# Bias and mask of two more attention units added to the scores by TensorE, with the bias tile kept in unused k slots

## The chip, the cores and the metric

One core of one Trainium2 chip runs the kernel. The metric is device microseconds (us) of one execution. Five things matter on a core: TensorE (PE in the profile, its weight loads PEld), VectorE (DVE), ScalarE (ACT), GpSimd (POOL, which here only issues loads), SyncE (SP, which issues stores and transposing DMAs), and the 16 DMA engines behind the queues.

## What is computed

Sliding-window attention with a linear distance bias (ALiBi), then a SwiGLU feed-forward block on its output. Eight sequences of 576 positions, 8 heads of 64, a window of 128:

```python
scores = scale * np.matmul(q, k.transpose(0, 1, 3, 2))
bias = slopes[:, None, None] * (-np.abs(rel).astype(np.float32))[None, :, :]
mask = (rel >= 0) & (rel < window)
scores = np.where(mask, scores + bias[None], -1000000000.0)
attn = softmax(scores)              # with 1e-9 added to the sum
x = (attn @ v).reshape(4608, 512)
out = (silu(x @ w_gate) * (x @ w_val)) @ w_out
```

The inputs q, k, v, the three weights (512x1536, 512x1536, 1536x512) and the output are float32; the loads that GpSimd issues turn them into fp16.

## The kernel before

**Attention in units.** A unit is a tile of 128 keys with the 256 queries that can see it, for all 8 heads; 36 units in all, nine for each pair of sequences (the ninth holds the last 64 positions of both). A unit goes through these steps:

- `load_qk`, `load_v` (L182 to L196): loads of its tiles, each called by its *rank*, issued by GpSimd in an order written out by hand for ranks up to 10 (L876 to L908). Ranks 9 and 10 stand at the end of it, behind the weights.
- `transposed` (L198): four TensorE transposes into PSUM (`pt`) and one copy to the tile's home, by VectorE for q, by ScalarE for k from rank 4 on. Home of a k tile is slot `rank % 12` of `kT` (L113), a tile of 12 slots of 128x512 fp16. Ranks from 11 on are transposed by DMA. Slot 11 is read as zeros by idle matmuls at the start (L115).
- `scores` (L243): for a unit 256 queries wide, eight matmuls of 64x256 into four PSUM banks (`ps`), four exponentials on ScalarE (`act`, L282) into `ex`, and two multiplications on VectorE (`mul`, L286) of 128x1024 each by `reg`, a tile that holds exp(-slope x distance), with 0 outside the window. Units 3, 7 and 8 are narrower and go through `scores_128` (L295, `psc`, `exc`).
- `weighted` (L325): matmuls of the exponentials with v and a column of ones (`av`), a reciprocal and a multiplication on VectorE (`x`).
- `x_transposed` (L358): four TensorE transposes (`px`) and a ScalarE copy into `xT`, the feed-forward block's input.

**The first units.** For the units below `FIRST = 4` (L29), bias and mask are not multiplied in behind the exponential. `first_masks` (L98) writes -slope x distance / scale (with a distance of 16000 outside the window) into the tile `bias`, 128 x 8 x 256 fp16, and `products` (L267) begins each of the four PSUM banks with a matmul of the identity `idm` and 512 columns of `bias` (L273), onto which the products of k and q are added. `early_tile` (L263) chooses between the two ways: with it, four matmuls of 128x512 more and no `mul`.

**Space.** `bias` comes from the pool `hpool` with the tag `hT`, two buffers: `stage` (first inputs and distances) takes the first, `bias` the second, and the feed-forward block's `hT` tiles follow in turn.

**Feed-forward in blocks** of 512 tokens. Block 0 holds units 0 to 3, block 1 units 4 to 7. For each of 12 column groups m, `wide` (L389) does four matmuls for the gate (`pg`) and four for the value (`pv`) into a ring of three PSUM buffers with the tag `gv`; `gate` (L407) is a tanh on ScalarE (`tt`) and one VectorE operation (`uu`); `val` (L419) one more on VectorE, into `hT`. A PSUM buffer of the ring is free again when VectorE has read it. The output product is `project` (`po`, L446, 12 matmuls) for block 0, and `strassen` with fewer products for later ones.

**Order.** Up to step 8 of the feed-forward block the order on TensorE, VectorE and ScalarE is the program's (L940); from there to step 60 a scheduler places each engine's instructions by its own estimate of when they can start; from step 60 TensorE's order is the program's again (L952). GpSimd's order is by hand throughout. Each engine executes its list in order.

Of the kernel before, what the change touches and what calls it, by code (L numbers as in the profile page):

```python
# [11 lines left out]
FP16 = mybir.dt.float16  # L12
# [4 lines left out]
P = 128  # L17
# [9 lines left out]
IDLE = {("k", 0): 0, ("q", 0): 2}  # L27
REPEAT = {("q", 1): 4, ("k", 1): 2}
FIRST = 4  # L29
LEAD = 6  # L30
PRE = 0
SEVEN_FROM = 6
# [19 lines left out]
def kernel(  # L52
# [11 lines left out]
    B, H, S, D = q.shape  # L64
# [10 lines left out]
    hpool = ctx.enter_context(tc.tile_pool(name="hp", bufs=2))  # L75
# [16 lines left out]
    reg = consts.tile([P, H, 256], FP16, name="m_reg")  # L92


    bias = hpool.tile([P, H, 256], FP16, name="bias", tag="hT")
    by_slot = sorted(range(H), key=slot)

    def first_masks():  # L98
# [14 lines left out]
    kT = consts.tile([P, NK, 4, P], FP16, name="kT")  # L113
    qT = consts.tile([P, NQ, 4, P], FP16, name="qT")
    idle = kT[:, NK - 1].rearrange("p j t -> p (j t)")  # L115
    nc.vector.memset(idle, 0.0)


# [51 lines left out]
    def transposed_home(name, rank):  # L170
        return kT[:, rank % NK] if name == "k" else qT[:, rank % NQ]
# [26 lines left out]
    def transposed(name, rank):  # L198

        if rank < FIRST:  # L200
            pt = ps_f.tile([P, 4, P], FP32 if (name, rank) in hw else FP16, name="pt",
# [14 lines left out]
        for _ in range(REPEAT.get((name, rank), 1)):  # L216
            for j in range(4):
                nc.tensor.transpose(pt[:, j, :], t_[:, 2 * j:2 * j + 2, :],
                                    idm if rank < FIRST else idm2)
        if name == "k" and rank >= FIRST:  # L220
            nc.scalar.copy(transposed_home(name, rank), pt)
# [21 lines left out]
    def scores(i):  # L243

        s, p = units[i]
        def combined(n):
            return scores_128(s, (3, 7, 8)[n], 8, (s, "c", n), msk[n])

        def together(one, two):
            return [one[0] + two[0]] + one[1:] + two[1:]  # L250

        if p == 8:
            first = combined(0) if s == 0 else []
            return first + together(combined(1), combined(2))
        if p == 7 and s == 0:
            return scores_128(s, p, p, (s, p), reg[:, :, 0:P])
        if p == 7:
            return together(scores_128(s, p, p, (s, p), reg[:, :, 0:P]), combined(0))
        if p == 3:
            return scores_128(s, p, p, (s, p), reg[:, :, 0:P], i < FIRST)  # L260
        ks = (9 * s + p) % NK
        banks = []
        early_tile = i < FIRST  # L263
        e = epool.tile([P, H, 256], FP16, name="ex", tag="ex", bufs=4)
        ex[(s, p)] = e

        def products():  # L267
            for q4 in range(2):
                two = [ps_a.tile([P, 2, 256], FP32, name="ps", tag="a") for _ in range(2)]
                banks.append(two)  # L270
                for par in range(2 if early_tile else 0):
                    o = 4 * q4 + 2 * par
                    nc.tensor.matmul(two[par], idm, bias[:, o:o + 2, :], start=True, stop=False)  # L273
                for j in range(2):
                    pair = 2 * q4 + j
                    for par in range(2):
                        rows = slice(64 * par, 64 * par + 64)
                        nc.tensor.matmul(two[par][:, j, :], kT[rows, ks, pair, :],  # L278
                                         qT[rows, p:p + 2, pair, :], start=(j == 0 and not early_tile),
                                         stop=(j == 1))  # L280

        def act(q4, par):  # L282
            o = 4 * q4 + 2 * par
            nc.scalar.activation(e[:, o:o + 2, :], banks[q4][par], AF.Exp, scale=scale)  # L284

        def mul(q4):  # L286
            if early_tile:
                return
            o = slice(4 * q4, 4 * q4 + 4)
            nc.vector.tensor_mul(e[:, o, :], e[:, o, :], reg[:, o, :])  # L290

        return [[products], [lambda: act(0, 0)], [lambda: act(0, 1), lambda: mul(0)],
                [lambda: act(1, 0)], [lambda: act(1, 1), lambda: mul(1)]]

    def scores_128(s, kt, qt, key, m, early_tile=False):  # L295

        ks = (9 * s + kt) % NK
        banks = []
        e = epool.tile([P, H, P], FP16, name="exc", tag="exc", bufs=5)
        ex[key] = e  # L300

        er4 = e.rearrange("k (a par b) q -> k a par b q", a=2, par=2)

        def products():
            banks.extend(ps_a.tile([P, 4, P], FP32, name="psc", tag="a") for _ in range(2))
            for par in range(2 if early_tile else 0):
                nc.tensor.matmul(banks[par].rearrange("k (a b) q -> k a b q", a=2), idm,
                                 bias.rearrange("k (a par b) q -> k a par b q", a=2, par=2)
                                 [:, :, par, :, 0:P], start=True, stop=False)
            for j in range(4):  # L310
                for par in range(2):
                    rows = slice(64 * par, 64 * par + 64)
                    nc.tensor.matmul(banks[par][:, j, :], kT[rows, ks, j, :], qT[rows, qt, j, :],  # L313
                                     start=(j == 0 and not early_tile), stop=(j == 3))

        def act(par):
            nc.scalar.activation(er4[:, :, par], banks[par].rearrange("k (a b) q -> k a b q", a=2),  # L317
                                 AF.Exp, scale=scale)

        return [[products], [lambda: act(0)],  # L320
                [lambda: act(1), lambda: early_tile or nc.vector.tensor_mul(e, e, m)]]
# [3 lines left out]
    def weighted(i):  # L325
# [4 lines left out]
        for half in range(2):  # L330
            pool, tag = (ps_f, "gv") if i < FIRST else (ps_a, "a")
            av = pool.tile([P, 4, D + 1], FP32, name="av", tag=tag)
# [51 lines left out]
    hT = {}  # L384
# [424 lines left out]
    def first_tiles():  # L809

        first_masks()
        transposes_to(need[0] + 1)
        for n, _ in enumerate(run(scores(0))):
            if n == 0:
                transposes_to(need[1])
        for i in range(FIRST):
            if i + 1 < FIRST:
                for n, _ in enumerate(run(scores(i + 1))):
                    if n == 0 and i + 2 < FIRST:
                        transposes_to(need[i + 2])  # L820
            weighted(i)

            if i >= 2:
                begin(4, i - 1)
            if i > 0:
                x_transposed(i - 1)
        begin(6, 2)
        begin(4, 3)
        gate(0, 0, early[(0, 0, "g")][0], 0, 384)
        x_transposed(FIRST - 1)  # L830
        val(0, 0, early[(0, 0, "v")][0], 0, 384)
        later_masks(0, 2)
        gate(0, 1, early[(0, 1, "g")][0], 0, 384)
        val(0, 1, early[(0, 1, "v")][0], 0, 384)
        begin(6, 3)

    def attention():
# [3 lines left out]
        for _ in run(scores(FIRST)):  # L841
            yield FIRST
# [93 lines left out]
    def everything():  # L936
# [13 lines left out]
        for step in steps:  # L950
# [3 lines left out]
            if step == MASKS_AT:  # L954
# [3 lines left out]

            lead = LEAD if done < X_DMA_FROM - 2 else LEAD + 4
            blk = (0 if step + LEAD < b1 else 1 if step + LEAD < 60  # L960
                   else min(NBLK - 1, 2 + int((step + lead - 60) // 34.5)))
# [43 lines left out]
```

## Time and profile before

| | us |
|---|---|
| median of the 4 runs shown (344.7 to 345.17) | 344.94 |
| the profiled execution | 344.89 |
| its span, first to last instruction | 343.1 |

The profile is of one execution; its span leaves out 1.79 us ahead of the first instruction and behind the last. TensorE's granted clock was 1.000 throughout.

| engine | busy us | share of the span |
|---|---|---|
| PE | 329.5 | 96% |
| DVE | 277.7 | 81% |
| ACT | 207.7 | 61% |
| POOL | 109.8 | 32% |

How to read it: in a *timeline* each row is a run of like instructions of one engine, with its start, its length, and in square brackets how long the engine had been idle ahead of it and who ended that. Matmuls are pipelined: one of 128x512 is shown with 0.38 us, and the next starts 0.216 us later, so gaps are found by counting from start to start. A row's `out<-in` gives the tiles by the program's names, and L with a number is the line of the kernel.

### The profile page before, as it was taken

What the parts mean: (1) busy time and instruction counts of PE and PEld (TensorE: products, weight loads), DVE (VectorE), ACT (ScalarE), POOL (GpSimd) and SP (SyncE); (2) the same over time, 40 slices, a digit from 0 to 9 for tenths busy, and PEclk for the clock granted to TensorE, in tenths of its full rate; (3) what the DMA queues carried; (4) which work ended last, traced back from release to release, by engine and by line L of the source; (5) the groups of instructions that cost most, each with busy time, mean ns of one, the idle gap of its engine ahead of it and who ended that gap; (6) DMA issues with size and microseconds to landing.
All of it is one profiled execution on the core that took longest, in us unless ns stands there. A gap on an engine that the chain in (4) does not pass through costs nothing.

```text
span 343.1 us, 7778 instructions
## 1 busy us (share of the span) xinstructions
PE 329.5 (96%) x2983; PEld 218.7 (64%) x2983; DVE 277.7 (81%) x652; ACT 207.7 (61%) x412; POOL 109.8 (32%) x136
## 2 busy tenths in 40 slices
PE   7999989999999999999999999999999999999995
PEld 4484455444456566556565655565788878888884
DVE  6578886999798679988899999999855875775683
ACT  3758676465666765756556547563467666776640
POOL 8968672648765176743017000000000000000000
PEclk9999999999999999999999999999999999999999
DMA  9999999999999999999949914021101101011014
GB/s 153 169 180 176 162 171 148 85 129 167 139 171 143 157 184 167 169 164 145 185 111 101 179 32 78 15 65 45 63 2 61 63 0 64 4 60 63 0 69 118
DMA packets 160037, 37.37 MB, mean 109 GB/s; under 512 B 147328, under 2 KB 155648, under 8 KB 160000
## 3 DMA queue, kind: packets, MB, share of 16 engines
q0 software_dynamic: 118336, 18.62, 81.8%
q1 hardware_dynamic: 40976, 17.64, 29.3%
q10 hardware_dynamic: 688, 0.62, 0.6%
q8 instruction: 23, 0.38, 0.5%
q14 instruction: 14, 0.11, 0.1%
HBM read 37.91 MB, written 9.44 MB: 138 GB/s over the span
## 4 chain that ended last, share of the span: by engine, by line
PE 67%; DVE 17%; DMA 4%; ACT 4%; POOL 3%; issue 3%; DVEq 0%; ACTq 0%; POOLq 0%
PE po L532 15%; PE pg L397 13%; PE pv L397 12%; PE gX L623 8%; PE gY L623 4%; PE av L345 3%; DVE uu L416 3%; PE p L532 3%; DMA wg_sb<-in_moe_w_gate_dram 3%; DVE hT L427 2%; PE po L451 2%; PE ps L278 2%; PE gZ L623 2%; DVE x L348 2%; DMA kn<-in_k_dram 2%
## 5 line engine op out<-in xcount | busy, mean ns | idle before, releaser
L397 PE MATMUL pv<-xT,wv_sb 128*128 128x512 f16 (+2 forms) x320 | 76.5, 358 | 0.6 <-DVE uu L416 0.3
L397 PE MATMUL pg<-xT,wg_sb 128*128 128x512 f16 (+2 forms) x320 | 75.8, 358 | 0.3 <-DVE xT L373 0.2
L415 ACT ACTIVATE tt<-pg 128x512 f16<-128x512 f32 (+2 forms) x70 | 41.3, 590 | 50.3 <-PE pg L397 49.4
L284 ACT ACTIVATE ex<-ps 128x512 f16<-128x512 f32 x96 | 50.0, 604 | 11.5 <-PE ps L278 11.5
L416 DVE SCALAR_TENSOR_TENSOR uu<-tt,pg 128x512 f16<-128x512 f16 (+2 forms) x69 | 45.9, 665 | 10.4 <-ACT tt L415 10.2
L427 DVE TENSOR_TENSOR hT<-uu,pv 128x512 f16<-128x512 f16 (+2 forms) x70 | 46.6, 666 | 3.6 <-PE pv L397 1.6
L185 POOL DMA_DIRECT2D va<-in_v_dram x40 | 34.4, 866 | 37.4 <-PE av L345 29.3
L397 PEld LDWEIGHTS <-wv_sb 128*128 128x128 f16 x320 | 28.3, 98 | 24.1 <-issue 3.0
L397 PEld LDWEIGHTS <-wg_sb 128*128 128x128 f16 x320 | 28.2, 98 | 24.3 <-issue 2.5
L532 PEld LDWEIGHTS <-hT 128*128 128x128 f16 x384 | 36.8, 98 | 10.4 <-issue 1.1
L191 POOL DMA_DIRECT2D kn<-in_k_dram x39 | 33.5, 861 | 18.6 <-DMA kT<-kn 11.2
L191 POOL DMA_DIRECT2D qn<-in_q_dram x39 | 33.6, 868 | 17.6 <-DMA va<-in_v_dram 9.4
L532 PEld LDWEIGHTS <-S 128*128 128x128 f16 x288 | 27.7, 98 | 10.6 <-issue 2.5
L290 DVE TENSOR_TENSOR ex<-ex,m_reg 128x1024 f16<-128x1024 f16 x42 | 28.6, 686 | 3.2 <-ACT ex L284 3.1
L348 DVE TENSOR_TENSOR x<-av,rec 128x256 f16<-128x256 f32 x72 | 28.5, 419 | 0.4
L532 PE MATMUL po<-T,S 128*128 128x256 f16 x192 | 26.5, 273 | 0.5 <-DVE S L487 0.5
L532 PE MATMUL po<-T,hT 128*128 128x256 f16 x192 | 26.1, 273 | 0.0
L317 ACT ACTIVATE exc<-psc 128x512 f16<-128x512 f32 x40 | 21.3, 607 | 4.1 <-PE psc L313 4.1
L675 DVE TENSOR_TENSOR hT<-s,v 128x512 f16<-128x512 f16 x18 | 7.6, 423 | 18.5 <-ACT s L674 18.5
L345 PEld LDWEIGHTS <-ex 128*128 128x128 f16 x384 | 17.4, 97 | 4.6 <-issue 1.3
L345 PE MATMUL av<-va,ex 128*128 128x65 f16 x384 | 19.3, 193 | 0.7 <-DMA kn<-in_k_dram 0.5
L278 PE MATMUL ps<-qT,kT 64*128 64x256 f16 x192 | 16.5, 272 | 0.4 <-DVE qT L223 0.2
(134 smaller groups left out, 536.2 us busy)
## 6 DMA issues: line engine op xcount, KB each, us to landing
out_dram<-osb SPq DMA_DIRECT2D x32, 256.0 KB, 2.5
va<-in_v_dram POOLq DMA_DIRECT2D x32, 128.0 KB, 8.3
qn<-in_q_dram POOLq DMA_DIRECT2D x31, 128.0 KB, 9.2
kn<-in_k_dram POOLq DMA_DIRECT2D x31, 128.0 KB, 9.2
wg_sb<-in_moe_w_gate_dram POOLq DMA_DIRECT2D x6, 256.0 KB, 7.6
wv_sb<-in_moe_w_val_dram POOLq DMA_DIRECT2D x6, 256.0 KB, 8.1
wo_sb<-in_moe_w_out_dram POOLq DMA_DIRECT2D x2, 768.0 KB, 9.6
kn<-in_k_dram POOLq DMA_DIRECT2D x8, 64.0 KB, 7.0
```

Source lines behind the costliest of these rows:

```text
L185: nc.gpsimd.dma_start(va[rank][p0:p1, :, 0:D], src)
L191: nc.gpsimd.dma_start(t_[p0:p1], src)
L284: nc.scalar.activation(e[:, o:o + 2, :], banks[q4][par], AF.Exp, scale=scale)
L290: nc.vector.tensor_mul(e[:, o, :], e[:, o, :], reg[:, o, :])
L345: nc.tensor.matmul(av[:, j, :], w, val, start=(n == 0), stop=(n == len(todo) - 1))
L348: nc.vector.tensor_mul(x[:, 4 * half:4 * half + 4, :], av[:, :, 0:D], rec.broadcast_to([P, 4, D]))
L397: nc.tensor.matmul(ps[:, c0:c1], w[:, kb, ms], xT[n][:, kb, c0:c1], start=(kb == 0 and c0 == 0), stop=(kb == NKB - 1 and c1 == 512), skip_ ...
L415: nc.scalar.activation(tt, pg[:, c0:c1], AF.Tanh, scale=0.5)
L416: nc.vector.scalar_tensor_tensor(out=uu, in0=tt, scalar=one if (n, m) == PIN else 1.0, in1=pg[:, c0:c1], op0=ALU.add, op1=ALU.mult)
L427: nc.vector.tensor_mul(hT[n][:, m, c0:c1], acted[(n, m)][1][:, c0:c1], pv[:, c0:c1])
L532: nc.tensor.matmul(dst, a[:, m, cols], b[:, m, :], start=(start and m == 0), stop=(m == HM - 1), skip_group_check=True)
L623: nc.tensor.matmul(dst[:, i, :], w[:, kb, c0 + i * P:c0 + (i + 1) * P], a[:, kb, :], start=(start and i == 0 and kb == 0), stop=(i == 1 an ...
```

## The change

The limit up to which 256-wide units take the bias by TensorE becomes 6 instead of 4, so units 4 and 5 do too (units 3 and 7 keep their own limit, `FIRST`). The bias tile leaves `hpool` and lies in slots 7 to 10 of `kT`, which no k tile uses before rank 7.

```diff
 FIRST = 4
+BIASED = 6
...
-    bias = hpool.tile([P, H, 256], FP16, name="bias", tag="hT")
     by_slot = sorted(range(H), key=slot)
...
     idle = kT[:, NK - 1].rearrange("p j t -> p (j t)")
+    bias = kT[:, 7:11].rearrange("p r j t -> p (r j t)").rearrange("p (h q) -> p h q", h=H)
     nc.vector.memset(idle, 0.0)
...
         ks = (9 * s + p) % NK
         banks = []
-        early_tile = i < FIRST
+        early_tile = i < BIASED
         e = epool.tile([P, H, 256], FP16, name="ex", tag="ex", bufs=4)
```

## Prediction

> **What bounds the kernel now.** I read the page first. TensorE is busy for nearly the whole span at full clock, so what is added to it counts unless it falls into a gap, and what is taken from VectorE counts only where TensorE waits for it.
>
> ```profile
> ## 1 busy us (share of the span) xinstructions
> PE 329.5 (96%) x2983; PEld 218.7 (64%) x2983; DVE 277.7 (81%) x652; ACT 207.7 (61%) x412; POOL 109.8 (32%) x136
> ```
>
> The change touches one stretch: the scores of units 4 and 5. The rows of the tiles give their place and the price of each operation: the multiplications of units 4 and 5 stand at 31.10, 32.30, 36.34 and 37.27 us, and the operation that replaces them has run twelve times at the start. The first row is VectorE's multiplication over the whole kernel (mean 686 ns), the second the bias matmul (377/379/390 ns).
>
> ```profile
> L290 DVE TENSOR_TENSOR ex<-ex,m_reg 128x1024 f16<-128x1024 f16 x42 | 28.6, 686 | 3.2 <-ACT ex L284 3.1
> ...
> L273 PE MATMUL ps<-bias,idm x12: 377/379/390, 8.7 to 14.3; 128*128 128x512 f16 x12
> ```
>
> Then the stretch in four windows that end at marks in TensorE's list: the end of the value matmuls of column group 8, the end of the gate matmuls of group 10, the start of block 1, and the point behind the last value matmuls ahead of unit 8's `av`. Columns: length, then busy time and count for each engine, clock, DMA share, GB/s.
>
> ```profile
> 27.97:39.47 11.50, 11.19 (x73) 5.27 (x73) 9.72 (x19) 8.75 (x17) 8.61 (x12) 1.00 1.97 174
> 39.47:44.29 4.82, 4.79 (x50) 2.42 (x48) 4.00 (x9) 3.63 (x7) 3.35 (x5) 1.00 1.82 137
> 44.29:56.59 12.30, 11.29 (x125) 6.40 (x124) 9.62 (x25) 8.58 (x17) 6.71 (x8) 1.00 1.65 171
> 56.59:66.44 9.85, 9.85 (x49) 4.02 (x48) 8.16 (x16) 5.15 (x10) 3.33 (x4) 1.00 1.16 91
> ```
>
> "Busy" hides small gaps, because a matmul is shown 0.38 us long while the next starts 0.216 us behind it (four `pg` matmuls take 0.86 us in the chain of waits). TensorE's timeline, counted from start to start, shows them:
>
> ```profile
> 27.11 1.02 PE L397 MATMUL pv<-xT,wv_sb 128*128 128x512 f16 x4 [0.28 <-DVE uu L416]
> 28.14 1.02 PE L397 MATMUL pg<-xT,wg_sb 128*128 128x512 f16 x4
> ...
> 31.37 1.03 PE L397 MATMUL pv<-xT,wv_sb 128*128 128x512 f16 x4
> 32.44 1.02 PE L397 MATMUL pg<-xT,wg_sb 128*128 128x512 f16 x4
> ...
> 33.74 0.81 PE L397 MATMUL pv<-xT,wv_sb 128*128 128x512 f16 x3
> 34.76 0.61 PE L278 MATMUL ps<-qT,kT 64*128 64x256 f16 x8 [0.21 <-DVE qT L223]
> ...
> 38.12 0.42 PE L345 MATMUL av<-va,ex 128*128 128x65 f16 x8
> 38.61 1.02 PE L397 MATMUL pv<-xT,wv_sb 128*128 128x512 f16 x4
> ```
>
> The gaps: 27.97 to 28.14 (0.17), 32.23 to 32.44 (0.21), 34.39 to 34.76 (0.37) and, behind eight `av` of 0.03 each, 38.36 to 38.61 (0.25). The reader is to see that these four come just where VectorE is late.
>
> **The change, part by part.** I follow the changed kernel's lists of instructions on each engine with the durations above.
>
> *Added:* 8 bias matmuls on TensorE at 0.216 us = 1.73 us (their weight loads, the identity, hide as those of `pg` do: 98 ns each, behind a cadence of 0.216). *Removed:* 4 multiplications on VectorE; one follows the next 0.60 us later, so 2.4 us. ScalarE keeps its four exponentials a unit.
>
> *27.97 to 39.47.* Gap 0.17: a bias matmul now stands in it, since it needs only a free bank: -0.17. A single `pv` at 29.00 is followed at 29.31 instead of 29.22; the order that did this is gone: -0.09. Gap 0.21: `pg` waited for its PSUM buffer, freed by `hT` L427 (31.70, ends 32.38), which stood behind the multiplication of 31.10; without it the buffer is free at about 32.03 and is wanted at 32.84: -0.21. Gap 0.37: `qT` was late behind the multiplication of 32.30; two bias matmuls now stand ahead of the products: -0.37. Gap 0.25: `uu` was late behind the multiplication of 37.27: -0.25. A new wait: k's copy for unit 5 stands behind a tanh on ScalarE, and TensorE reaches unit 5's products 0.25 us before it is done: +0.25. Behind that wait stand the rest of the products and unit 5's exponentials; VectorE has room there now. Sum: 1.73 - 0.17 - 0.09 - 0.21 - 0.37 - 0.25 + 0.25 = +0.89 at the end of the window.
>
> *39.47 to 44.29.* Work by start-to-start times: 12 wide matmuls 2.59, 16 `av` 0.48, 8 `ps` 0.54, 4 `px` 0.22, 8 `pt` 0.44: 4.27 of 4.82, so 0.55 us of gaps, mostly unit 6's products waiting for copies of k and q. In the new order four gate matmuls stand between those transposes and the products and cover the copies. I take -0.53 (bounds 0 and -0.55). Delay at this mark: +0.36.
>
> *44.29 to 56.59.* 24 wide matmuls 5.18, 12 `px` 0.66, 24 `pt` 1.32, 32 `psc` 1.3, 32 `av` 0.96: 9.42 of 12.30, so some 2.9 us of gaps: here a chain from unit to unit paces TensorE, and one could hope for more from a relieved VectorE. But look at its end. First the loads of q for ranks 9 and 10 (issued at 44.0 and 44.8), then TensorE:
>
> ```profile
> L191 POOL DMA_DIRECT2D qn<-in_q_dram x2: 896/900/903, 44.0 to 44.8; - x2
> ...
> DMA to landing us min/median/max: 11.0/11.0/11.0
> ```
>
> ```profile
> 55.65 0.28 PE L371 MATMUL px<-idm,x 128*128 128x128 f16 x2
> 55.88 0.40 PE L218 MATMUL pt<-idm,qn 128*128 128x128 f16 x4
> 56.11 0.59 PE L451 MATMUL po<-wo_sb,hT 128*128 128x512 f16 x2
> 56.59 1.02 PE L397 MATMUL pg<-xT,wg_sb 128*128 128x512 f16 x4
> ```
>
> The two land at about 54.98 and 55.85, and their transposes start at 54.98 and 55.88, each behind a gap of 0.12 to 0.14. TensorE waits for the **load**, not for VectorE. These loads wait for earlier loads: POOL's waits end half a microsecond behind a landing, also where the page names an engine (`wg_sb` issued at 19.25 landed 8.4 later, at 27.65, and POOL went on at 28.21, put down to PE; `va` from 33.12 landed at 42.0, and the second `wo_sb` went out at 42.29). So nothing in the change moves them. In the changed list those transposes still stand ahead of block 1. Without waits TensorE would come to them at 55.76 + 0.36, less two `po` matmuls that stand ahead of them before and behind them after: 55.76 + 0.36 - 0.43 = 55.69. That is before 55.85, so **the earlier gains and losses are cut off at the landing**. Behind it stand 4 `pt` (0.22) and 3 `po` (0.65) instead of 2: block 1 begins at 55.88 + 0.87 = 56.75, 0.16 later than 56.59. The twelfth `po` matmul has moved behind block 1's first groups, to about 66.4: another 0.22. Together **+0.38 us**.
>
> *Behind that.* 56.59 to 66.44 has TensorE busy 9.85 of 9.85, and VectorE's waits there end with ScalarE's reading of TensorE, so the delay is passed on. VectorE is busy 29.6 of the 30 us from 60 to 90, with the same work before and after; the delay reaches it through the exponentials (its wait of 0.22 at 66.96), so I count nothing as absorbed (bounds 0 and -0.38).
>
> *Space.* The bias lies where k tiles of ranks 7 to 10 come later; rank 7's copy stands at 46.80 us on ScalarE, 11 us behind unit 5's last product. Cost 0. The `hT` tiles swap buffers; the first, `stage`, is read for the last time at 25.85 us and rewritten by block 1 near 59 us. Cost 0.
>
> Two rules of the Trainium skill, page "TensorE: Matmul & The Clock Gate", speak to the price, and the sum does not use them. Section "Part 3: Packing small matmuls — row/col tiling" says that a weight load overlaps matmuls in flight only if it goes to other rows of the array; by that the eight identity loads of 98 ns would add 0.78 us, but the full-array `pg` matmuls here keep 0.216 with a load each. Section "Back-to-back issue gap" gives about 131 ns a matmul of 512 columns in a sustained stream; by that the eight would cost 1.05 instead of 1.73, but no stream of this trace runs faster than 0.216.
>
> **The sum.** 344.89 for the profiled execution + 0.38 = 345.27; on the median of the runs, 0.05 higher, 345.32. I say 345.3.
>
> **Rivals.**
>
> *The matmuls come through (slower).* The cover fails: gaps do not close, and TensorE reaches rank 10's q transposes after 55.85. With no gap closed it arrives at 55.76 + 1.73 - 0.43 = 57.06, 1.2 late, total +1.6: 346.5. It decides once less than about 1.2 us of gaps close ahead of 55.85; I counted 1.37 by 44.29, a thin margin. For it: VectorE's and ScalarE's order change too, and the 2.9 us of gaps from 44.29 can come out either way. Half way: 346.0.
>
> *The relief is carried on (faster).* If the landing is not what holds TensorE at 55.88, the 2.4 us taken from VectorE could come through the chain of units 6 and 7: at most 2.4 - 0.43 = 2.0 us, 342.9; half of it is 343.9. Against it: VectorE idles 1.54 us at 58.29 and 1.06 at 52.08, so it has no backlog that relief would shorten, and two waits that end at landings to within 0.03 us are hardly chance.
>
> *It does nothing:* the bias tile in `kT` costs a wait, or the gaps in the stretch up to 90 us take the 0.38. 344.9 to 345.0.
>
> **Chances.** A measurement tells 0.2% (0.69 us) from no change: within 344.25 to 345.63. The forecast 0.50 (its own range 344.9 to 345.9, of it 0.42 within, 0.08 above), the matmuls come through 0.31, relief 0.14, nothing 0.05. So faster 0.14, same 0.47, slower 0.39. The range leaves out the relief case and the far end of the slow one: 344.5 to 346.4.
>
> **What would show it.** Right: TensorE's gaps at 32.2, 34.4 and 38.4 gone, `pt<-qn` of rank 10 still starting at about 55.9, `pg` of block 1 at 56.7 to 56.8, VectorE with 38 multiplications. Wrong: these transposes well behind the landing (the first rival), or the load landing at another time, or block 1 starting before 56.4 (the second). A difference that first appears behind 66 us would contradict all of it.

## The result and the profile after

The changed kernel takes 345.58 us (median of 35 runs, 345.27 to 347.0), the kernel before 345.08 beside it (53 runs): ratio **1.0017**, 95% interval 1.0013 to 1.0022, so 0.6 us slower, between 0.4 and 0.8. The profiled execution takes 345.47, with a span of 343.7 (before: 344.89 and 343.1), and the clock was 1.000 in both. In the changed kernel every line number behind the edit is higher by 1.

The page of the kernel after shows what was added and removed: 8 matmuls more, 38 multiplications instead of 42. VectorE's busy time falls by 2.1 us.

```profile
PE 331.5 (96%) x2991; PEld 219.4 (64%) x2991; DVE 275.6 (80%) x648; ACT 207.7 (60%) x412; POOL 109.8 (32%) x136
...
L291 DVE TENSOR_TENSOR ex<-ex,m_reg 128x1024 f16<-128x1024 f16 x38 | 25.9, 686 | 3.1 <-ACT ex L285 3.0
```

Two of the four windows in the kernel after (length, then busy time and count of PE, PEld, DVE, ACT, POOL). TensorE is now busy 11.43 of 11.50 in the first one and 12.14 of 12.30 in the third of the prediction's windows, where it had 0.31 and 1.01 idle.

```profile
27.97:39.47 11.50, 11.43 (x68) 4.76 (x67) 6.59 (x12) 8.38 (x16) 8.69 (x12) 1.00 1.97 175
...
44.29:56.59 12.30, 12.14 (x143) 7.06 (x140) 10.54 (x26) 9.51 (x19) 7.43 (x9) 1.00 1.66 170
```

TensorE's timeline of the kernel after, over units 4 and 5 (L274 are the bias matmuls, L279 the products of q and k):

```profile
29.06 0.38 PE L274 MATMUL ps<-kT,idm 128*128 128x512 f16 x1
29.37 0.39 PE L279 MATMUL ps<-qT,kT 64*128 64x256 f16 x4
29.69 0.60 PE L274 MATMUL ps<-kT,idm 128*128 128x512 f16 x2
30.23 0.39 PE L279 MATMUL ps<-qT,kT 64*128 64x256 f16 x4
30.56 1.04 PE L398 MATMUL pv<-xT,wv_sb 128*128 128x512 f16 x4
...
34.90 0.38 PE L398 MATMUL pv<-xT,wv_sb 128*128 128x512 f16 x1
35.35 0.39 PE L279 MATMUL ps<-qT,kT 64*128 64x256 f16 x4
...
40.04 1.02 PE L398 MATMUL pv<-xT,wv_sb 128*128 128x512 f16 x4
```

The first value matmuls in that stretch start at 27.12 in both kernels; those of group 8 at 40.04 instead of 38.61. **At 40 us the change has cost 1.42 us**, not the 0.89 of the forecast. The single `pv` of 34.90 should be followed at 35.12 and is at 35.35: the new wait for k's copy, 0.23. And two steps in the rows say where the rest is: one bias matmul from 29.06 takes until 29.37, 0.31 instead of 0.216; two from 29.69 until 30.23, 0.54 instead of 0.43. A full-array matmul that is followed by products of 64 rows costs 0.10 more here than one followed by its like. It is not a wait for one late copy: the same 0.31 stands ahead of the narrower products further on (`pv` at 50.01, `psc` at 50.32).

Ahead of block 1 stand the transposes and the `po` matmuls:

```profile
55.72 0.74 PE L219 MATMUL pt<-idm,qn 128*128 128x128 f16 x5
56.30 0.81 PE L452 MATMUL po<-wo_sb,hT 128*128 128x512 f16 x3
56.94 1.03 PE L398 MATMUL pg<-xT,wg_sb 128*128 128x512 f16 x4
```

Block 1 starts at 56.94 instead of 56.59, **+0.35** (forecast 56.75). So 1.07 of the 1.42 us came back between 40 and 57 us; 0.22 of that is the twelfth `po` matmul, which now stands behind this mark, and 0.85 is time regained. Of these five transposes four are rank 10's; five take 0.28, here 0.58 pass until `po`, so 0.3 us of waiting lies among them. The chain that ended last names it (start, length, what): q of rank 10, issued at 45.56, lands at 56.02, and its transposes start at 56.06.

```profile
45.56 10.46 DMA qn<-in_q_dram
56.02 0.05 issue
56.06 0.40 PE pt L219 x4
```

From block 1's start to the end of the span it is 286.76 us, before 286.51: +0.25, where the twelfth `po` matmul now stands.

So three questions: what do the added matmuls cost and why; what gave 1.07 us back, VectorE's relief or something else; and does the landing decide?

### The profile page after: what moved, and what is told of

The parts are those of the page before. It is cut to its first block, busy times and chain, and to the rows that moved or that the text cites. A ratio compares the mean times of both kernels' runs of the same rounds, so it can differ in the third digit from the quotient of the medians.

```text
span 343.7 us, 7789 instructions
## 1 busy us (share of the span) xinstructions
PE 331.5 (96%) x2991; PEld 219.4 (64%) x2991; DVE 275.6 (80%) x648; ACT 207.7 (60%) x412; POOL 109.8 (32%) x136
## 4 chain that ended last, share of the span: by engine, by line
PE 68%; DVE 16%; DMA 7%; ACT 3%; issue 3%; POOL 1%; ACTq 0%; DVEq 0%; POOLq 0%
PE po L533 15%; PE pg L398 12%; PE pv L398 12%; PE gX L624 8%; PE gY L624 4%; PE av L346 3%; DMA qn<-in_q_dram 3%; DMA va<-in_v_dram 3%; DVE uu L417 3%; PE po L452 3%; PE ps L279 3%; PE p L533 2%; PE gZ L624 2%; DVE hT L428 2%; DVE x L349 1%
## 5 line engine op out<-in xcount | busy, mean ns | idle before, releaser
L291 DVE TENSOR_TENSOR ex<-ex,m_reg 128x1024 f16<-128x1024 f16 x38 | 25.9, 686 | 3.1 <-ACT ex L285 3.0
L279 PE MATMUL ps<-qT,kT 64*128 64x256 f16 x192 | 16.6, 273 | 0.2
```

The costliest lines, as they stand in the source:

```text
L279: nc.tensor.matmul(two[par][:, j, :], kT[rows, ks, pair, :], qT[rows, p:p + 2, pair, :], start=(j == 0 and not early_tile), stop=(j == 1))
```

## The experiments

The table gives the median, that of the kernel before measured beside it, and the ratio with its 95% interval. The ratio is not that of the two medians (for e5_no_matmuls these would give 0.9992), and verdicts go by its interval. Edits are to the kernel after unless said otherwise. M is the start of group 8's value matmuls, B that of block 1, in the profiled execution; "to M" counts from the first value matmuls of the stretch (27.11 in the kernel before), so that it leaves out how late the stretch began.

| run | median | before | ratio | to M | M to B |
|---|---|---|---|---|---|
| kernel before | | | | 11.50 | 17.98 |
| kernel after | 345.58 | 345.08 | 1.0017 (1.0013 to 1.0022) | 12.92 | 16.90 |
| e1_space_only | 345.10 | 345.16 | 0.9996 (0.9985 to 1.0008) | 11.11 | 18.20 |
| e2_both_ways | 345.80 | 345.16 | 1.0013 (1.0002 to 1.0025) | 12.92 | 16.71 |
| e3_after_v8late | 345.70 | 345.16 | 1.0018 (1.0004 to 1.0033) | 12.92 | 16.70 |
| e4_after_v9early | 347.40 | 345.16 | 1.0054 (1.0034 to 1.0075) | 12.93 | 17.82 |
| e5_no_matmuls | 344.93 | 345.20 | 1.0002 (0.9983 to 1.0020) | 11.06 | 18.11 |
| e6_before_v8late | 345.04 | 345.20 | 0.9996 (0.9987 to 1.0004) | 11.12 | 17.84 |
| e7_limit_5 | 346.00 | 345.20 | 1.0019 (1.0011 to 1.0028) | 12.10 | 17.84 |
| e8_first_v8late | 346.15 | 345.20 | 1.0025 (1.0016 to 1.0034) | 12.39 | 16.82 |
| e9_unit5_only | 346.23 | 345.03 | 1.0025 (1.0013 to 1.0037) | 12.35 | 18.05 |
| e10_unit5_first | 344.93 | 345.03 | 1.0000 (0.9987 to 1.0012) | 11.84 | 16.95 |
| e11_after_first45 | 345.43 | 345.03 | 1.0007 (0.9998 to 1.0016) | 12.39 | 16.83 |
| e12_unit5_v8late | 344.93 | 345.02 | 0.9990 (0.9977 to 1.0004) | 12.35 | 16.85 |

### Space alone

```diff
-BIASED = 6
+BIASED = 4
```

> The bias tile lies in slots 7 to 10 of kT, but only units 0 to 3 use it: the limit is 4 again. My theory (the matmuls cost, the space costs nothing): the time of the kernel before, 345.1 us, within 0.1. Rival (the bias tile among the k tiles, or the other turn of the hT buffers, adds a wait): up to 0.5 us more, the whole difference. The load of q for rank 10 should land at 55.85 as before; if it lands 0.2 later, as in the changed kernel, that delay belongs to the space or to chance and not to the matmuls.

Ratio 0.9996: the bias tile in `kT` costs nothing that can be told. The profile has the waits of the kernel before. One thing is of use later: its block 1 starts at 56.86, 0.27 later than in the kernel before, with the same list of TensorE, since the loads of q landed later (rank 10's transposes start at 56.10 instead of 55.88). One profile's landing is not a constant, and a landing 0.2 later does not need the added matmuls.

### Matmuls and multiplications both

```diff
         def mul(q4):
-            if early_tile:
+            if i < FIRST:
                 return
```

> The changed kernel, but units 4 and 5 are multiplied by their masks as well, so VectorE keeps its four multiplications (the bias then counts twice in the scores of these two units). TensorE's list is that of the changed kernel, instruction by instruction. My theory (the four multiplications held TensorE up by some 0.8 us ahead of 40 us, and TensorE reaches the transposes of rank 10's q only 0.3 us ahead of their load): TensorE is about 0.8 us later there, 0.5 of it behind the landing, so 346.1 us. Rival (relief of VectorE is worth nothing because of the landing): 345.6, as the changed kernel. Rival (VectorE's 2.4 us count in full): 347.5 or more.

The measured ratio, 1.0013, is no worse than that of the kernel after, and my figure of 346.1 was too high. TensorE's list is that of the kernel after, matmul by matmul, and its timeline shows why: this execution starts the stretch 0.60 us later (q of rank 5 landed late), and then every row stands 0.60 behind the kernel after, group 8 included (40.64 and 40.04), though VectorE makes the four multiplications here.

```profile
27.72 1.03 PE L398 MATMUL pv<-xT,wv_sb 128*128 128x512 f16 x4
...
40.64 1.02 PE L398 MATMUL pv<-xT,wv_sb 128*128 128x512 f16 x4
```

So **with the matmuls in place VectorE's relief gains nothing that can be told**: the added matmuls themselves fill the gaps, and up to group 8 VectorE is then not what TensorE waits for. The same list also came out with VectorE's work unchanged, so it is not the relief that brings the new order. And a list without gaps hands a late load on in full; in the run with space alone, a wait of 0.68 us in the same place is made good by 38.66.

### Neither matmuls nor multiplications

```diff
-                for par in range(2 if early_tile else 0):
+                for par in range(2 if i < FIRST else 0):
...
-                                         qT[rows, p:p + 2, pair, :], start=(j == 0 and not early_tile),
+                                         qT[rows, p:p + 2, pair, :], start=(j == 0 and not i < FIRST),
```

Units 4 and 5 go without bias and mask here.

> Units 4 and 5 get neither the bias matmuls nor the multiplications, so their scores have no bias and no mask: VectorE's relief alone, 2.4 us off it. TensorE's list is nearly that of the kernel before. My theory, after the run that kept both ways (TensorE's timeline was the same with and without the multiplications): relief closes the gaps at 32.2, 34.4 and 38.4 us here, since no matmuls fill them, but TensorE then waits for the landing of rank 10's q at about 56, so the total is that of the kernel before, 345.1, at best 0.2 less. Rival (VectorE's relief counts once it is not paid for with matmuls): 0.8 to 2.4 us less, 342.7 to 344.3.

Ratio 1.0002, with an interval that would hide 0.6 us. Relief alone gains 0.44 us up to group 8 (from 27.57 to 38.63, 11.06 instead of 11.50) and nothing that can be told in the end. From group 8 on TensorE's list here is neither the old one nor that of the kernel after: the old one's waits for `x` and `xT` are gone, but `psc` waits 0.64 us for `qT` (50.45) and the transposes of rank 9's q 0.36 us for their load (55.13), so M to block 1 takes 18.11 us. What relief would gain with another order behind it, no run shows.

### The loads of q earlier or later

```diff
-    load(8)
+    load_qk(8)
...
     load_qk(10, "q")
+    load_v(8)
```

> The changed kernel with one move in GpSimd's list: the loads of v for rank 8, wanted only at 66 us, stand behind those of rank 9 and of rank 10's q instead of ahead of them, so that these land about 1 us earlier. TensorE's list is unchanged. My theory (TensorE waits 0.3 us for the landing of rank 10's q): block 1 begins 0.3 us earlier, total 345.3 us. Rival (the wait at 56 us is only where the profile puts it, and TensorE is held by VectorE or ScalarE there): no change, 345.6.

> The kernel before with the loads of v for rank 8 behind those of rank 9 and rank 10's q. My theory (the kernel before waits for these two landings, 0.12 to 0.14 us each in its profile, up to 0.6 together in others): 0.3 us less, 344.8. The difference to the changed kernel with the same move then grows to 0.9. Rival (the landings hold nothing, as one could read the same move in the changed kernel): no change, 345.1.

And the other way, v of rank 9 moved ahead of q of rank 10:

> The changed kernel with the opposite move: the load of v for rank 9 stands ahead of that of rank 10's q, so that the latter lands about 0.9 us later. TensorE's list is unchanged. My theory: TensorE starts block 1 later by the same 0.9 us, total 346.5 us. Rival (the landing does not hold TensorE): no change, 345.6.

Later loads hurt: 1.0054, and in the profile TensorE waits 1.05 us for q of rank 10, whose transposes start at 57.22, with block 1 at 58.10. Earlier loads gain nothing that can be told, neither on the kernel after (345.70; an interval this wide would hide 0.5 us) nor on the one before (0.9996, though block 1 starts at 56.46 and no load is waited for ahead of it). In the profile of the first the five transposes do take 0.28 (57.82, then `po` at 58.10), so the wait of 0.3 us is gone; from the value matmuls near 24.5 that wait for `hT` to block 1 it is 32.26 us instead of 32.46 (0.1 of the gain goes again between `po` and block 1, 0.75 instead of 0.64). My gain of 0.3 is not confirmed: it is 0.2 in the profile and unresolved in the time. (The profiled execution of that run began 2.1 us later, so only distances within it are used.)

### One unit instead of two

```diff
-BIASED = 6
+BIASED = 5
```

> The changed kernel with the limit 5: only unit 4 takes its bias by matmul, four of them, and two multiplications go. Behind unit 4 TensorE's list is that of the kernel before, with all twelve output matmuls of block 0 ahead of block 1. My theory (what TensorE loses is swallowed by gaps that VectorE's and ScalarE's answers leave, and by the landing): 0 to 0.15 us more than before, 345.1 to 345.25. Rival (each matmul counts): half of the changed kernel's 0.6, 345.4.

**A miss for both theories**: four matmuls cost as much as eight (1.0019 and 1.0017). M is at 39.52 (+0.91 against before; 0.31 of it a late load at 27.19, 0.60 the matmuls), and from there to block 1 it is 17.84, as in the kernel before with its loads moved (17.84); nothing comes back. Its timeline has, at the same places and of the same size, the three waits that the kernel before has and the kernel after has not. First this run:

```profile
50.13 0.28 PE L372 MATMUL px<-idm,x 128*128 128x128 f16 x2 [0.57 <-DVE x L349]
...
51.06 0.28 PE L372 MATMUL px<-idm,x 128*128 128x128 f16 x2 [0.20 <-DVE x L349]
...
52.02 0.38 PE L314 MATMUL psc<-qT,kT 64*128 64x128 f16 x7 [0.20 <-ACT xT L376]
```

The kernel before:

```profile
49.22 0.28 PE L371 MATMUL px<-idm,x 128*128 128x128 f16 x2 [0.57 <-DVE x L348]
...
50.15 0.28 PE L371 MATMUL px<-idm,x 128*128 128x128 f16 x2 [0.20 <-DVE x L348]
...
51.11 0.38 PE L313 MATMUL psc<-qT,kT 64*128 64x128 f16 x7 [0.20 <-ACT xT L375]
```

The kernel after, where matmuls stand in between and the profile marks no wait (from start to start 0.18 us is left ahead of the second `px`, at 49.88):

```profile
48.28 0.59 PE L398 MATMUL pg<-xT,wg_sb 128*128 128x512 f16 x2
48.72 0.28 PE L372 MATMUL px<-idm,x 128*128 128x128 f16 x2
```

The three waits are 0.97 us as the profile marks them. With a limit of 5 the scheduler's list behind unit 4 stays the old one: value matmuls of group 11 early (three at 47.57), then nothing left to put into units 6 and 7's waits. In the kernel after it spreads the gate and value matmuls of groups 10 and 11 singly and in pairs between `px`, `psc` and `av`, and the waits are filled but for that 0.18. So I formed a new theory: **what came back is the new order, not VectorE's time**. It needs a run with the new order and fewer matmuls.

### Unit 5 alone

```diff
-        early_tile = i < BIASED
+        early_tile = i < FIRST or i == 5
```

> Only unit 5 takes bias and mask by TensorE; unit 4 keeps its multiplications. The scheduler's list of TensorE is that of the kernel before up to unit 5's products and that of the kernel after from column group 8 to block 1: the counterpart of the run with unit 4 alone, with the same four bias matmuls. My theory (the loss ahead of 40 us is paid by the matmuls, the gain between 40 and 56 us comes from the list there): value matmuls of group 8 some 0.5 to 0.8 us later than before, then about 1.0 us back, so that rank 10's q transposes are held by the landing as in the kernel before and block 1 starts at 56.6 to 56.9; 344.9 to 345.3 beside 345.2 for the kernel before. Rival (four matmuls cost what they cost, wherever they stand, and no list gives anything back): as the run with unit 4 alone, block 1 at 57.3, 345.8 to 346.0.

TensorE's own part came out as the theory has it: M at 39.61 (+0.85 against before after taking off a start 0.15 later), no waits for `x` or `xT`, and k's transposes ahead of block 1 at 54.77, 0.43 earlier than in the kernel after. The time did not: 346.23 (median of 6 runs), above even the rival's figure. The rows ahead of block 1:

```profile
54.77 0.39 PE L219 MATMUL pt<-idm,kn 128*128 128x128 f16 x4
55.91 0.34 PE L219 MATMUL pt<-idm,qn 128*128 128x128 f16 x3 [0.75 <-DMA qn<-in_q_dram]
...
56.77 0.40 PE L219 MATMUL pt<-idm,qn 128*128 128x128 f16 x4 [0.35 <-DMA qn<-in_q_dram]
...
57.66 1.03 PE L398 MATMUL pg<-xT,wg_sb 128*128 128x512 f16 x4
```

The loads of q were issued at 44.31 and 45.17, earlier than in the kernel after, and took 11.6 us instead of 10.5. TensorE, early, waited 1.1 us for them. The two accounts are then separated by moving the loads and nothing else:

```diff
         early_tile = i < FIRST or i == 5
...
-    load(8)
+    load_qk(8)
...
+    load_v(8)
```

> The run with unit 5 only (bias and mask of unit 5 by TensorE, of unit 4 by VectorE), all lists as there, but the loads of v of rank 8 stand behind the last loads of q. In that run TensorE waited for the two q loads at 55.91 and 56.77 and block 1 started at 57.66; without these waits its list would reach block 1 at about 56.4. If the landing alone made the run with unit 5 only slow, and the four matmuls and the list do not: no wait for q ahead of block 1, block 1 at 56.3 to 56.6, 345.0 to 345.2. Rival (the landing is only where a loss shows that TensorE's work has anyway): 345.8 or more.

344.93, ratio 0.9990: **1.3 us less than the same lists with the loads in the old order** (1.2 by the two ratios, whose intervals lie apart). Block 1 stands at 56.31, as expected. Not all of the wait is gone, though: these five transposes would take 0.28 and take 0.53, so 0.25 us is left (q of rank 10, issued at 44.3, lands 11.1 later).

```profile
55.14 0.69 PE L219 MATMUL pt<-idm,qn 128*128 128x128 f16 x5
55.67 0.81 PE L452 MATMUL po<-wo_sb,hT 128*128 128x512 f16 x3
56.31 1.03 PE L398 MATMUL pg<-xT,wg_sb 128*128 128x512 f16 x4
```

M to block 1 is 16.85 here, 16.71 with matmuls and multiplications both, 16.90 in the kernel after; with the old order 17.84 where no load is late. Of that difference of about 1.0 us 0.22 is the moved `po` matmul. Unit 4 alone keeps the old order and gets nothing back, though M is 0.91 later there than in the kernel before, so lateness by itself does not close the waits; unit 5 alone brings the new one with the same four matmuls; and with both matmuls and multiplications it is the same, so VectorE's load does not matter. Why the same loads took 11.6 us in one list and 11.1 in the other is open.

### Fewer changes between wide and 64-row matmuls

All four bias matmuls of a unit in a row, then the eight products, so that each unit changes over once instead of twice (with the loads of v of rank 8 moved, too):

```diff
+            for q4 in range(2):
+                two = banks[q4]
                 for j in range(2):
```

> The changed kernel with the v loads of rank 8 late, and with the four bias matmuls of a unit all ahead of its eight products, instead of two ahead of each four. So TensorE changes once a unit from matmuls on 128 rows to those on 64 rows, not twice; each change costs some 0.1 us at its beginning and 0.05 at its end in the changed kernel's timeline. My theory (no gap is left in the changed kernel up to 40 us, so TensorE itself sets the pace, and with the earlier landing nothing cuts it off): 0.3 us less than the same kernel with the old order (345.7), so 345.4. Rival (something else sets the pace there): 345.7.

A miss: 346.15. The edit also reordered units 0 to 3, and the start is 0.95 us later for it (the mark of 24.48 stands at 25.43). From that mark to group 8 it is 15.03 against 15.56 of the same kernel with the bias matmuls in their old order, so the part in question did what it should; but a run that loses elsewhere proves little. So once more with units 4 and 5 only, loads moved too:

```diff
+            def biases(q4):
                 for par in range(2 if early_tile else 0):
...
+            if i >= FIRST:
+                biases(0)
+                biases(1)
+            for q4 in range(2):
+                two = banks[q4]
+                if i < FIRST:
+                    biases(q4)
                 for j in range(2):
```

> The kernel after with the four bias matmuls of units 4 and 5, and of these alone, in one row ahead of the eight products, and with the loads of v of rank 8 behind the last loads of q. The first units keep their order, so the start is that of the kernel after. If a change between 128-row and 64-row matmuls costs about 0.10 us one way and 0.05 the other: group 8's value matmuls about 0.3 to 0.5 us earlier than in the kernel after, and 345.2 to 345.4 beside 345.6 for the kernel after. Rival (the changes cost nothing, something else made the 0.5 us): 345.6 to 345.7.

345.43, just above the range that I expected; the ratio, 1.0007, is 0.0011 below that of the run with the same loads and the old order of the bias matmuls, and the two intervals overlap. The timeline is plainer. From the first value matmuls to group 8 it is now 12.39 us (27.55 to 39.94) instead of 12.92, **0.53 less** with the same matmuls:

```profile
29.49 0.81 PE L275 MATMUL ps<-kT,idm 128*128 128x512 f16 x3
30.23 0.61 PE L287 MATMUL ps<-qT,kT 64*128 64x256 f16 x8
30.77 1.04 PE L406 MATMUL pv<-xT,wv_sb 128*128 128x512 f16 x4
```

Three bias matmuls take 0.74 to the products (0.65 and one 0.09 for the change), eight products 0.54. Not all of the 0.53 is the price of changes. In unit 4, where nothing waits, it is 0.22: 1.28 us from 29.49 to 30.77, where the kernel after takes 1.50 (29.06 to 30.56). In unit 5 it is 0.31, of which 0.10 lies in the products (one row of eight for two of four) and 0.21 in the wait for k's copy, which two bias matmuls now fill (`pv` at 35.12 is followed at 35.36, not 0.45 us later).

Both remedies on the kernel with unit 5 alone:

> As the run with unit 5 only, with unit 5's four bias matmuls in one row ahead of its eight products (two changes between full-array and 64-row matmuls fewer) and the loads of v of rank 8 behind the last loads of q, which lets those of q land about 1 us earlier. If the changes cost what I read (some 0.25 us a unit) and the landing is what still holds TensorE: no wait for the landing, block 1 at 56.2 to 56.5, 344.7 to 344.9 beside 345.2 for the kernel before. Rival (TensorE's own work sets the time, the landing does not): no better than the run with unit 5 only.

344.93, no better than with the loads alone (344.93): block 1 at 56.28 and 56.31. The landing still holds TensorE a little: the five transposes ahead of `po` take 0.50 where they would take 0.28. Unit 5 waits for q's copy anyway (0.17 to 0.21), so the order of its matmuls saved 0.13 (group 8 at 39.33 and 39.46). My 0.25 for one unit held only where nothing else waits.

No version can be told from the kernel before as faster; the lowest, unit 5 alone with the loads moved, is level with it within its interval (0.9977 to 1.0004).

## Why the prediction was right, and where its steps failed

The total (+0.38 forecast; +0.58 in the profiled executions, +0.50 in the medians) and its sign are right, and the rival of matmuls that come through in full (+1.6) did not happen. But two large steps were wrong and a third effect, which had no term, made up for them: TensorE was 0.53 us later at 40 us than forecast, got nothing back by the next mark where 0.53 was forecast, and then regained most of both. That its arrival at the transposes came out within 0.1 us of the forecast is luck.

**27.97 to 39.47, "+0.89": +1.42.** Failed in size. The matmuls (1.73), the gaps of 0.17, 0.21, 0.37 and 0.25 (the last 0.23) and the new wait (0.25; 0.23) came as written. Missing was the price of changing to 64-row products and back: about 0.10 at each change to them and 0.05 for each row of only four, so 0.31 in unit 4 and 0.21 in unit 5, where the first change lies inside the wait for k's copy. That is 0.52, the whole difference. The "gap" of 0.09 at 29.22, "the order that did this is gone", was such a change already, a wide matmul with products behind it: it stood in the trace of before, and I read it as idle time.

**Why the gaps closed.** I tied three of them to VectorE being late (`hT`, `qT`, `uu`). The run with both shows that they close without relief: the matmuls take the time in which VectorE's results come. Same number, other cause; the cause matters, since it says that relief gives no more once the matmuls are there.

**39.47 to 44.29, "I take -0.53": nothing.** Failed. The gate matmuls of group 10 end at 45.7 instead of 44.29, still 1.4 late. The new order did cover the copies, but an `av` waits there from 43.81 to 44.12.

**44.29 to 56.59, no term but the cut at the landing:** failed as a mechanism. I saw 2.9 us of gaps there and counted none of them as changed. Part of the 2.9 was not idle either: three `po` matmuls between rows of 64-row products take 0.32 us each (51.42 to 52.72), not 0.216. The waits for `x` and `xT`, 0.57 + 0.20 + 0.20, go through the scheduler's new order. Counted from M to block 1, with all that was lost and gained between, 0.85 us is regained, and 0.22 more is the `po` matmul that moved out. 1.42 - 0.85 is 0.57, the difference of the profiled executions (0.58). The changed lists were there to be read; I followed them for two windows and stopped.

**The landing.** "TensorE waits for the load" is right: 0.3 us in the kernel after, 1.1 in two variants, and 1.3 us between two runs that differ in the order of the loads alone. "So nothing in the change moves them" is right to 0.2 us: rank 10 landed at 56.02 instead of 55.85. The second `wo_sb` was issued at 43.01 instead of 42.29, behind a `va` that took 9.65 instead of 8.9; but with space alone the transposes started 0.2 us late as well, so whether the change moved the landing at all is open. The cut came about as forecast, but for the kernel after the landing isn't what makes it slower than before: without the wait its time did not fall measurably. Unforced, it arrives at 55.78 (forecast 55.69), so close to the landing that either limit gives almost the same end.

**Block 1 at 56.75, then 0.22 for the twelfth `po`:** 56.94, and 0.25 between the two profiles. Over all profiles, the nine with the moved `po` need 286.75 us from block 1's start to the end on average, the five without 286.62: 0.13, with a scatter of 0.1. Direction right, size not settled.

**Space 0, nothing absorbed behind 66 us:** nothing speaks against either (0.9996, 0.9985 to 1.0008; the loss at block 1 is found at the end).

The 0.10 for a change goes with one rule of the Trainium skill, page "TensorE: Matmul & The Clock Gate", section "Part 3: Packing small matmuls — row/col tiling": a weight load is pulled ahead of a matmul in flight if it goes to rows that this one doesn't use, or into a background weight buffer. In the trace of the kernel after, the loads stand ahead of their matmuls except at the changes: behind another full-array matmul the identity's load at 28.84 is 0.22 us ahead of its matmul (29.06), but the first product's load starts at 29.36, with the product itself (29.37), and the identity's next load at 29.69, with its matmul (29.69). Whether the late load is the whole 0.10 was not tested.

## What to carry to other kernels

Where an engine is busy 96%, price an added instruction by the time from start to start in its real neighbourhood: a full-array matmul ahead of 64-row products cost 0.31 us here, not 0.216, and putting like beside like took 0.22 us off a unit in which nothing else waits. Work taken from an engine is worth something only if someone still waits for it once the replacement is in place; a run that does both shows that at once. When a scheduler makes the lists, read the new list through to the next point that the edit can't move (here a load's landing), waits included: here its by-product (0.85 us regained) was larger than what VectorE's relief gained by itself (0.44 us up to group 8).

## What was not expected of the hardware

- Changing from 128x512 full-array matmuls to 64-row products takes about 0.10 us (29.06 to 29.37 for one matmul), and a row of four products 0.32 us where half of eight would be 0.27.
- Loads of 128 KB issued in the same order by GpSimd take 10.5 to 11.6 us from run to run and list to list; q of rank 5 made TensorE wait 0.43 to 0.74 us in six profiles and not at all in the eight others. Gaps in a list absorb this; a list without gaps passes it on (0.60 us at 27.72 is still 0.60 at 53.95 in the run with both).
- Moving v of rank 8 (two loads of 64 KB) behind the last loads of q was worth 1.3 us where TensorE had arrived early, and nothing measurable where it had not.
